# Splitting the last step of a weight conversion: rounding or storing two attention steps after the sign

## The chip, the cores and the metric

The kernel runs on one core of a Trainium2 chip. The core has a matrix engine (PE, TensorE), a vector engine (DVE, VectorE), a scalar engine (ACT, ScalarE), a general engine (POOL, GpSimd) and a queue that issues DMA transfers (SP, SyncE). Each engine runs its own instructions in the order in which the program emits them, and waits for other engines through semaphores. The metric is the device time of one launch in microseconds.

## The reference

Inputs are eight batches with eight heads, 576 positions and 64 features per head. The reference has three stages, all in float32:

```python
# 1. linear attention with positive features, per batch and head
proj = einsum('bhsd,df->bhsf', x, w_phi); proj -= max(abs(proj), axis=-1)
phi  = concat([exp(proj), exp(-proj)])
num  = phi(q) @ (phi(k).T @ v);  den = phi(q) . sum(phi(k)) + 1e-6
x    = num / den
# 2. causal convolution gate with 5 taps
x    = (sigmoid(conv5(x, conv_w)) * (x @ w_val)) @ w_out
# 3. Fourier mixing, layer norm, two-layer network
u    = x + real(fft2(x));  un = (u - mean) / sqrt(var + 1e-6)
out  = u + relu(un @ w_ch1) @ w_ch2
```

The weights `w_val`, `conv_w`, `w_out`, `w_ch1` and `w_ch2` arrive as float64 and are needed as float32 values, which the kernel makes on the chip from the two 32-bit halves of each number.

## The kernel before

The attention is cut into 16 units (a pair of batches and a pair of heads), each into five groups of 64-row or 128-row chunks, so 80 steps. `run_attention` (L1162) writes out one step after another by hand, and each step works on several groups at once: the projections of group `st` on PE (`emit_P`, L204, tile `pj`), the maximum and subtraction of group `st - 1` on DVE (`emit_Y`, L211 and L214), the key exponentials of group `st - 1` on ACT (`emit_kE`, L222 and L223, tile `ke`), the key-value products of group `st - 2` on PE (`emit_KV`, L243, tile `kv`), and so on. What is emitted first runs first on its engine. The third group of a unit is half as large; its projections show as `x8` instead of `x16`, so two such rows in succession are five steps apart.

Between these, the steps of the weight conversions are taken (`todo`). There are 21 pieces: two of `w_val` (tiles `wv`), two of `w_out` (`wo`), the small one of the taps, and 16 of `w_ch1` and `w_ch2`. One piece is a generator, `convert`, with four steps. The first loads the float64 numbers (L86, tile `raw`, two buffers). The second takes the exponent bits on DVE (L94) and the low half on ACT (L95). The third takes the high mantissa bits on DVE (L97, tile `mt`, two buffers), scales the exponent on ACT (L98) and does two operations on POOL (L99, L100). The fourth makes the sign on ACT (L102), multiplies twice on POOL (L103, L104) and calls `done`. For `w_val` and `w_out`, `done` rounds on ACT (L66, reading what L104 wrote) and subtracts on POOL (L75); for `w_ch1` and `w_ch2` it is a store on SP (L326, tile `w_scr`); for the taps a small copy on POOL (L347).

The four steps of piece `i` run at its start step plus 0, 3, 4 and 6, which is the table `lead`. The start is `i * (X_AT - 2 - lead[-1]) // 20`, with `X_AT` = 72, so `i * 64 // 20`: 0, 3, 6, 9, 12, 16, 19, 22 and so on to 64.

After the attention follow the gate and the Fourier mixing (batch by batch), and the two-layer network, whose order a planner chooses from its own costs.

Of the kernel before, what the change touches and what calls it, by code (L numbers as in the profile page):

```python
# [29 lines left out]
def f32(ap):  # L30
    return ap.bitcast(F32)
# [3 lines left out]
def attention_moe_mixer_kernel(  # L35
# [48 lines left out]
    def convert(i, src, n, shape, halve, done):  # L84
        raw = P["xf"].tile([128, 1024, 2], I32, tag="xf", name="raw64")[:, 0:n]
        nc.sync.dma_start(out=raw.rearrange("p n t -> p (n t)").rearrange("p (k f) -> p k f", k=shape[0]), in_=src)  # L86
        yield
        lo32, hi32 = raw[:, :, 0].bitcast(U32), raw[:, :, 1]
        a = P["xh"].tile([128, 2, 1024], I32, tag=f"x{i % 2}", name="cv")
        ex, lo = a[:, 0, 0:n], f32(a[:, 1, 0:n])  # L90
        sg = lo
        mt = stg.tile([128, 1024], I32, tag="mt", name="mt")[:, 0:n]
        w = f32(mt)
        nc.vector.tensor_scalar(out=ex, in0=hi32, scalar1=0x7FF00000, scalar2=None, op0=ALU.bitwise_and)  # L94
        nc.scalar.activation(out=lo, in_=lo32, func=ACTF.Copy, scale=2.0 ** -32)  # L95
        yield
        nc.vector.tensor_scalar(out=mt, in0=hi32, scalar1=0xFFFFF, scalar2=0x4B000000, op0=ALU.bitwise_and, op1=ALU.bitwise_or)  # L97
        nc.scalar.activation(out=ex, in_=ex, func=ACTF.Relu, scale=8.0, bias=ebias[:, int(halve):int(halve) + 1])  # L98
        nc.gpsimd.tensor_scalar(out=w, in0=w, scalar1=-7340032.0, scalar2=None, op0=ALU.add)  # L99
        nc.gpsimd.tensor_tensor(out=w, in0=lo, in1=w, op=ALU.add)  # L100
        yield
        nc.scalar.activation(out=sg, in_=hi32, func=ACTF.Sign)  # L102
        nc.gpsimd.tensor_tensor(out=w, in0=w, in1=f32(ex), op=ALU.mult)  # L103
        nc.gpsimd.tensor_tensor(out=w, in0=w, in1=sg, op=ALU.mult)  # L104
        done(w.rearrange("p (k f) -> p k f", k=shape[0]))
        yield

# [85 lines left out]
    def emit_P(i):  # L193
        u, g = divmod(i, NG)
        cs = GROUPS[g]
        n = len(cs)
        t = raw[u][0]
        pj[i] = p = ps_pj.tile([128, 2, 512], F32, tag="pj", name="pj")
        for w in range(2):
            for j, c in enumerate(cs):  # L200
                for h in range(2):
                    r = slice(64 * h, 64 * h + 64)
                    o = (w * n + j) * F
                    mm(p[:, h, o:o + F], t[r, w, 128 * c:128 * c + 128], wp[r, :], start=True, stop=True)  # L204

    def emit_Y(i, x):
        n = len(GROUPS[i % NG])
        pv = pj.pop(i)[:, :, 0:2 * n * F].rearrange("p h (c f) -> p h c f", f=F)
        m = sm_p.tile([128, 2, 2 * n], F32, tag="m", name="m")
        y = y_p.tile([128, 2, 2 * n, F], F32, tag="y", name="y")  # L210
        nc.vector.tensor_reduce(out=m, in_=pv, axis=AX.X, op=ALU.max, apply_absolute_value=True)  # L211
        if x is not None:
            emit_X(x)
        nc.vector.tensor_tensor(  # L214
            out=y, in0=pv, in1=m.unsqueeze(3).to_broadcast([128, 2, 2 * n, F]), op=ALU.subtract
        )
        yq[i] = y
# [40 lines left out]
    def emit_yT(i):  # L258
        n = len(GROUPS[i % NG])
        y = yq.pop(i)  # L260
        t = ps_tr.tile([128, 2, n, 128], F32, tag="tr", name="yt")
        for h in range(2):
            for j in range(n):
                nc.tensor.transpose(t[:, h, j, :], y[:, h, n + j, :], ident)
        e = qe_p.tile([128, 2, 2, n, 128], F32, tag="qe", name="qe")
        nc.scalar.activation(out=e[:, 0], in_=t, func=ACTF.Exp)
        nc.scalar.activation(out=e[:, 1], in_=t, func=ACTF.Exp, scale=-1.0)
        qE[i] = e
# [29 lines left out]
    def emit_XT(i):  # L298
        u, g = divmod(i, NG)
        bp, hp = divmod(u, 4)  # L300
        cs = GROUPS[g]
        n = len(cs)
        x = xs.pop(i)
        t = ps_tr.tile([128, n, 128], F32, tag="tr", name="xt")
        for j in range(n):
            nc.tensor.transpose(t[:, j, :], x[:, j].rearrange("p h d -> p (h d)"), ident)
        if g == 0:
            xT[u] = xT_p.tile([128, 2 * S], F32, tag="xT", name="xT")
        o = xT[u][:, 128 * cs[0]:128 * (cs[0] + n)]
        nc.scalar.activation(out=o, in_=t.rearrange("p c s -> p (c s)"), func=ACTF.Copy)  # L310
        if g == NG - 1:
            for b in range(2):
                nc.sync.dma_start(out=x_scr[2 * bp + b][hp], in_=xT[u][:, b * S:(b + 1) * S])
            xT.pop(u)
# [98 lines left out]
    def tap_steps(b, m):  # L413
        x = xf[b]
        if "psa" in P:
            acc = P["psa"].tile([128, 2, 512], F32, tag="pa", name="acc")[:, :, 0:HS]
        else:
            acc = P["g"].tile([128, 2, HS], F32, tag="acc", name="acc")

        def shifted(t):  # L420
            return x[:, m, t:t + S].rearrange("p (a s) -> p a s", a=2)
        nc.scalar.activation(out=acc, in_=shifted(4), func=ACTF.Copy, scale=cw[:, m, 4:5])  # L422
        for t in range(4):
            nc.vector.scalar_tensor_tensor(  # L424
                out=acc, in0=shifted(t), scalar=cw[:, m, t:t + 1], in1=acc, op0=ALU.mult, op1=ALU.add
            )
            if t < 3:
                yield
        taps[b, m] = acc
        yield  # L430

    def emit_taps(b, m):
        drain(tap_steps(b, m))
# [459 lines left out]
    def chain(*gens):  # L893
        for g in gens:
            yield from g
# [264 lines left out]


    def run_attention():  # L1162
        lead = (0, 3, 4, 6)
        todo = {}
        tap0 = chain(tap_steps(0, 0), tap_steps(0, 1))
        taps_at = (TOT - 4, TOT - 3, TOT - 2, TOT - 1, TOT, TOT, TOT + 1, TOT + 1)
        for i in range(len(pieces)):
            for l in lead:
                todo.setdefault(i * (X_AT - 2 - lead[-1]) // (len(pieces) - 1) + l, []).append(pieces[i])
        n_t = 2 * len(tables)  # L1170
        did_t = 0
        with tc.manual_schedule():
            for st in range(TOT + 6):
                u, g = divmod(st, NG)

                def at(lag):
                    return 0 <= st - lag < TOT

                if at(2):
                    emit_yT(st - 2)  # L1180
                if at(7) and st < TOT + 2:
                    emit_XT(st - 7)
                if at(0):
                    emit_P(st)
                if at(1):
                    emit_Y(st - 1, st - 6 if at(6) else None)
                elif st == TOT + 1:
                    emit_X(st - 6)
                if at(6) and st > TOT:
                    emit_XT(st - 6)  # L1190
                for c in todo.get(st, ()):
                    next(c)
                if at(1):
                    emit_kE(st - 1)
                if at(2):
                    emit_KV(st - 2)
                    emit_kvT(st - 2)
                for _ in range(taps_at.count(st)):
                    next(tap0)
                if at(5):  # L1200
                    emit_num(st - 5)
                    if st > TOT:
                        emit_X(st - 5)
                if g == (1 if u else 0) and u + 1 < NU:
                    load_kq(u + 1)
                if g == 2 and u + 1 < NU:
                    load_v(u + 1)
                while did_t < n_t and did_t * (X_AT - 5) < (st - 3) * n_t:
                    next(tables[did_t // 2])
                    did_t += 1  # L1210
                if st == X_AT:
                    assert did_t == n_t
                    load_x(0)
                    load_x(1)
                if 0 <= st - X_AT - 4 < 4:
                    split_x(0, (st - X_AT - 4,))
                if st == TOT + 1:
                    early.close()
                    open_mix()
                if 1 <= st - TOT < 5:  # L1220
                    emit_V(0, st - TOT - 1)
                    if st - TOT in (1, 3):
                        emit_taps(0, (st - TOT + 3) // 2)
# [145 lines left out]
```

## Time and profile before

| | |
|---|---|
| median of 3 runs | 1435.16 us (1435.16 to 1440.01) |
| the profiled execution | 1437.34 us, its span 1435.5 us |
| busy: PE, DVE, ACT, POOL | 94%, 87%, 57%, 49% |
| attention, 0 to 312 us | PE busy 286.16 us of 312 |
| the rest, 312 to 1435.5 us | PE busy 1060.96 us of 1123.5 |

A timeline row gives the start, the duration, the engine, the line, the operation with output and inputs, the sizes and the count of equal instructions that were merged; in square brackets stands the idle time of the engine just before, and the instruction that ended it. A row of the table by stretches gives, for each engine, its busy time and (in brackets) its number of instructions, then the granted PE clock as a share of 2.4 GHz, the share of time in which the DMA engines were busy, and the rate.

### The profile page before, as it was taken

To read this page: it belongs to the slowest core of one execution; us is meant where nothing else is said; L and a number is where in the kernel's file an instruction comes from. 1 tells how busy PE (TensorE), PEld (TensorE's weight loads), DVE (VectorE), ACT (ScalarE), POOL (GpSimd) and SP (SyncE) were. 2 spreads that over 40 slices of the span, in tenths; PEclk is the share of its full clock that TensorE was granted. 3 is DMA by queue.
4 is the path that set the end of the run, shared out by engine and by line. 5 is a ranking of instruction groups with operands and counts; after the bars stand their busy time and mean duration, and the time that the engine had idled before them with its cause. 6 is when DMAs were issued, how large, how long until landed. Compare 5 with 4: busy or idle time off the path is not lost.

```text
span 1435.5 us, 35040 instructions
## 1 busy us (share of the span) xinstructions
PE 1347.1 (94%) x14672; PEld 1297.1 (90%) x14672; DVE 1242.7 (87%) x1938; ACT 814.7 (57%) x1513; POOL 706.0 (49%) x526
## 2 busy tenths in 40 slices
PE   6899999997999999986899899999999999999998
PEld 6788888886999999976799899999999999999998
DVE  6689989876899999797999999999899887788876
ACT  5778888764545545464555554555465555444442
POOL 3858887732667666563555555545425111111111
PEclk9899999999999999998999999999999999999999
DMA  6347777741334433336323232222332222222211
GB/s 244 137 182 256 273 266 278 245 169 41 133 133 144 144 134 107 109 109 212 121 82 118 90 111 82 96 97 89 123 124 97 89 74 78 71 89 89 89 40 50
DMA packets 89851, 186.98 MB, mean 130 GB/s; under 512 B 10455, under 2 KB 37335, under 8 KB 87518
## 3 DMA queue, kind: packets, MB, share of 16 engines
q1 hardware_dynamic: 88488, 181.33, 37.2%
q10 hardware_dynamic: 1206, 3.41, 0.6%
q8 instruction: 115, 1.88, 0.5%
q14 instruction: 42, 0.34, 0.1%
HBM read 121.79 MB, written 62.93 MB: 129 GB/s over the span
## 4 chain that ended last, share of the span: by engine, by line
PE 43%; DVE 30%; POOL 9%; issue 8%; ACT 5%; DMA 4%; SPq 0%; ACTq 0%; DVEq 0%; POOLq 0%
PE cx L875 9%; PE x L806 9%; PE cy L875 5%; PE y L806 4%; DVE acc L424 4%; DVE A L647 3%; DVE c L647 3%; PE z L806 3%; PE kv L243 2%; DVE acc L647 2%; PE cz L875 2%; DMA raw<-in_w_ch_dram 2%; DVE s L751 2%; PE nm L282 2%; PE pj L204 2%
## 5 line engine op out<-in xcount | busy, mean ns | idle before, releaser
L875 PE MATMUL cx<-h,w 128*128 128x256 f32 x1152 | 176.2, 286 | 4.8 <-ACT h L66 2.5
L875 PEld LDWEIGHTS cx<-h,w 128*128 128x128 f32 x1152 | 158.3, 194 | 6.7 <-ACT h L66 3.1
L66 ACT ACTIVATE h<-c 128x512 fp32r<-128x512 f32 x180 | 111.6, 627 | 38.6 <-DVE c L647 22.2
L647 POOL TENSOR_TENSOR c<-c,c 128x512 f32<-128x512 f32 x35 | 49.7, 1421 | 167.9 <-ACT h L650 128.2
L647 DVE TENSOR_TENSOR acc<-cx,acc 128x512 f32<-128x512 f32 x144 | 98.1, 681 | 32.9 <-PE cx L875 32.2
L650 ACT ACTIVATE c<-c 128x512 f32<-128x512 f32 x108 | 67.9, 630 | 100.6 <-DVE c L647 99.3
L806 PE MATMUL x<-un,w 128*128 128x256 f32 x864 | 117.0, 285 | 7.6 <-DVE eo L647 6.9
L875 PE MATMUL cy<-h,w 128*128 128x256 f32 x864 | 117.3, 284 | 4.6 <-DVE h L72 1.9
L75 POOL TENSOR_TENSOR h<-c,h 128x512 fp32r<-128x512 f32 x33 | 48.1, 1459 | 148.9 <-ACT h L66 148.7
L806 PEld LDWEIGHTS x<-un,w 128*128 128x128 f32 x864 | 109.9, 193 | 8.2 <-issue 7.1
L424 DVE SCALAR_TENSOR_TENSOR acc<-xf,cw,acc 128x576 f32<-128x576 f32 x128 | 105.0, 820 | 11.9 <-ACT acc L422 10.6
L875 PEld LDWEIGHTS cy<-h,w 128*128 128x128 f32 x864 | 108.9, 191 | 7.0 <-DVE h L72 2.5
L243 PE MATMUL kv<-vraw,ke 128*64 128x66 f32 x2560 | 97.6, 230 | 14.6 <-ACT ke L222 9.8
L243 PEld LDWEIGHTS kv<-vraw,ke 128*64 128x64 f32 x2560 | 85.1, 141 | 26.2 <-ACT ke L222 13.2
L72 DVE TENSOR_TENSOR h<-c,h 128x512 fp32r<-128x512 f32 x111 | 104.2, 940 | 1.3 <-ACT h L66 0.7
L211 DVE TENSOR_REDUCE m<-pj 128x8 f32<-128x1024 f32 (+1 forms) x80 | 88.7, 1108 | 10.6 <-PE pj L204 10.6
L204 PE MATMUL pj<-wp,kqraw 64*128 64x128 f32 x1152 | 89.4, 294 | 5.7 <-DMA kqraw<-in_k_dram 4.9
L204 PEld LDWEIGHTS pj<-wp,kqraw 64*128 64x128 f32 x1152 | 73.8, 194 | 19.6 <-issue 18.1
L214 DVE TENSOR_TENSOR y<-pj,m 128x1024 f32<-128x1024 f32 (+1 forms) x80 | 88.7, 1109 | 0.4
L282 PE MATMUL nm<-kvT,qe 128*64 128x65 f32 x2304 | 84.4, 225 | 2.8 <-issue 1.3
L75 POOL TENSOR_TENSOR ge<-gs,ge 128x580 fp32r<-128x580 f32 x32 | 46.7, 1460 | 76.1 <-ACT ge L66 76.1
L99 POOL TENSOR_SCALAR mt<-mt 128x1024 f32<-128x1024 f32 (+1 forms) x21 | 55.6, 2650 | 57.4 <-DVE mt L97 47.3
(249 smaller groups left out, 4222.4 us busy)
## 6 DMA issues: line engine op xcount, KB each, us to landing
raw<-in_w_ch_dram SPq DMA_DIRECT2D x16, 1024.0 KB, 8.2
wr<-w_scr SPq DMA_DIRECT2D x32, 448.0 KB, 3.4
vraw<-in_v_dram SPq DMA_DIRECT2D x16, 660.0 KB, 9.3
x_scr<-xT SPq DMA_DIRECT2D x32, 288.0 KB, 6.5
xf<-x_scr SPq DMA_DIRECT2D x8, 1152.0 KB, 5.9
out_dram<-acc SPq DMA_DIRECT2D x36, 256.0 KB, 2.2
kqraw<-in_k_dram SPq DMA_DIRECT2D x15, 576.0 KB, 8.3
kqraw<-in_q_dram SPq DMA_DIRECT2D x15, 576.0 KB, 7.4
```

Source lines behind the costliest of these rows:

```text
L66: nc.scalar.activation(out=dst, in_=src, func=ACTF.Copy)
L72: nc.vector.tensor_tensor(out=dst, in0=src, in1=f32(hi), op=ALU.subtract)
L75: nc.gpsimd.tensor_tensor(out=dst, in0=src, in1=f32(hi), op=ALU.subtract)
L204: mm(p[:, h, o:o + F], t[r, w, 128 * c:128 * c + 128], wp[r, :], start=True, stop=True)
L211: nc.vector.tensor_reduce(out=m, in_=pv, axis=AX.X, op=ALU.max, apply_absolute_value=True)
L214: nc.vector.tensor_tensor(out=y, in0=pv, in1=m.unsqueeze(3).to_broadcast([128, 2, 2 * n, F]), op=ALU.subtract)
L243: mm(t[p, w, :], e[:, a, h, j, p], tv[:, h, slot, :], start=slot % 5 == 0 and w == 0, stop=slot % 5 == 4 and w == 3, skip_group_check=True)
L282: mm(t[p, 2 * j + h, 0:65], e[:, a, h, j, p], kt[:, 2 * h + a, b, :], start=(a == 0), stop=(a == 1))
L424: nc.vector.scalar_tensor_tensor(out=acc, in0=shifted(t), scalar=cw[:, m, t:t + 1], in1=acc, op0=ALU.mult, op1=ALU.add)
L647: op(e, cols, lambda e: (nc.vector if e == "v" else nc.gpsimd).tensor_tensor(out=o, in0=x, in1=y, op=alu), r, w)
L806: mm(p[:, n], l, v[:, kt], start=first and n + kt + m == 0, stop=kt == 1 and m == 2, skip_group_check=True)
L875: mm(p[:, o], v, r[:, n], start=first and o + n + m == 0, stop=n + m == 3, skip_group_check=True)
```

## The change

The call of `done` gets a step of its own, two attention steps behind the step that makes the sign, and `lead` grows by an entry.

```diff
@@ convert @@
         nc.scalar.activation(out=sg, in_=hi32, func=ACTF.Sign)
         nc.gpsimd.tensor_tensor(out=w, in0=w, in1=f32(ex), op=ALU.mult)
         nc.gpsimd.tensor_tensor(out=w, in0=w, in1=sg, op=ALU.mult)
+        yield
         done(w.rearrange("p (k f) -> p k f", k=shape[0]))
         yield
@@ run_attention @@
-        lead = (0, 3, 4, 6)
+        lead = (0, 3, 4, 6, 8)
```

Since `lead[-1]` is in the formula for the start steps, these become `i * 62 // 20`: 0, 3, 6, 9, 12, 15, 18, 21, 24, 27, 31 and so on to 62. The first five are as before; later pieces start up to two steps earlier, and their last step stays at 70 at the latest. The order of instructions on PE is the same in both kernels.

On ACT, at steps 6 to 8 (the sign of piece 0 is L102 of `raw_226`; lines below L105 count one more in the changed kernel). Before:

```order
L102 ACTIVATE cv<-raw_226 128x1024
L66 ACTIVATE wv_147<-mt 128x1024
L95 ACTIVATE cv<-raw_311 128x1024
L222 ACTIVATE ke<-y 128x512
L223 ACTIVATE ke<-y 128x512
L66 ACTIVATE sq<-tab 128x580
L266 ACTIVATE qe<-yt 128x512
```

On ACT, the same place in the changed kernel:

```order
L102 ACTIVATE cv<-raw_226 128x1024
L95 ACTIVATE cv<-raw_311 128x1024
L223 ACTIVATE ke<-y 128x512
L224 ACTIVATE ke<-y 128x512
L66 ACTIVATE sq<-tab 128x580
L267 ACTIVATE qe<-yt 128x512
L268 ACTIVATE qe<-yt 128x512
L311 ACTIVATE xT<-xt 128x256
L98 ACTIVATE cv<-cv,ebias 128x1024
L223 ACTIVATE ke<-y 128x512
L224 ACTIVATE ke<-y 128x512
L267 ACTIVATE qe<-yt 128x512
```

The rounding `wv<-mt` no longer stands between the sign and the next two key exponentials; it comes 13 instructions later, in step 8.

On POOL, from the first piece on, before (L99 to L104 are the arithmetic of one piece, L75 the subtraction behind the rounding):

```order
L99 TENSOR_SCALAR mt<-mt 128x1024
L100 TENSOR_TENSOR mt<-cv,mt 128x1024
L103 TENSOR_TENSOR mt<-mt,cv 128x1024
L104 TENSOR_TENSOR mt<-mt,cv 128x1024
L75 TENSOR_TENSOR wv_148<-mt,wv_147 128x1024
L99 TENSOR_SCALAR mt<-mt 128x1024
L100 TENSOR_TENSOR mt<-cv,mt 128x1024
L103 TENSOR_TENSOR mt<-mt,cv 128x1024
```

On POOL, the same place in the changed kernel:

```order
L99 TENSOR_SCALAR mt<-mt 128x1024
L100 TENSOR_TENSOR mt<-cv,mt 128x1024
L103 TENSOR_TENSOR mt<-mt,cv 128x1024
L104 TENSOR_TENSOR mt<-mt,cv 128x1024
L99 TENSOR_SCALAR mt<-mt 128x1024
L100 TENSOR_TENSOR mt<-cv,mt 128x1024
L75 TENSOR_TENSOR wv_148<-mt,wv_147 128x1024
L103 TENSOR_TENSOR mt<-mt,cv 128x1024
```

The subtraction of one piece has moved behind the first two operations of the next.

On SP, where the stores of the third and fourth piece of `w_ch1` and `w_ch2` stand, before:

```order
L326 DMA w_scr_73<-mt 128x2x512
L86 DMA raw_2024<-in_w_ch_dram 128x2x1024
L313 DMA x_scr_67<-xT 128x576
L313 DMA x_scr_68<-xT 128x576
L326 DMA w_scr_74<-mt 128x2x512
```

On SP, the same two stores in the changed kernel:

```order
L86 DMA raw_1962<-in_w_ch_dram 128x2x1024
L191 DMA vraw<-in_v_dram 128x1320
L327 DMA w_scr_73<-mt 128x2x512
L314 DMA x_scr_67<-xT 128x576
L314 DMA x_scr_68<-xT 128x576
L86 DMA raw_2242<-in_w_ch_dram 128x2x1024
L186 DMA kqraw<-in_k_dram 128x1152
L186 DMA kqraw<-in_q_dram 128x1152
L354 DMA tab<-in_feat_tab_dram 128x516
L327 DMA w_scr_74<-mt 128x2x512
```

Each store now stands behind the load of the piece after next, and not ahead of it.

## Rows read from the trace of the kernel before

**Rows 1.** The page, part 1: busy us, share of the span, instructions.
```profile
PE 1347.1 (94%) x14672; PEld 1297.1 (90%) x14672; DVE 1242.7 (87%) x1938; ACT 814.7 (57%) x1513; POOL 706.0 (49%) x526
```
**Rows 2.** Table by stretches; columns: stretch, length, PE, PEld, DVE, ACT, POOL, clock, DMA.
```profile
21.80:82.85 61.05, 50.54 (x993) 44.87 (x992) 41.47 (x72) 42.76 (x79) 49.85 (x23) 0.92 0.36 127
34.14:38.50 4.36, 4.18 (x59) 3.59 (x60) 1.21 (x4) 4.36 (x9) 4.28 (x3) 0.67 0.67 272
49.14:53.00 3.86, 3.73 (x65) 3.47 (x65) 0.16 (x1) 3.79 (x7) 3.86 (x2) 0.56 0.23 89
...
85.85:295.36 209.51, 202.54 (x4372) 181.23 (x4371) 189.36 (x323) 174.13 (x330) 162.23 (x67) 1.00 0.74 258
276.83:295.36 18.53, 18.34 (x404) 16.61 (x403) 15.70 (x30) 14.64 (x30) 10.80 (x6) 1.00 0.51 183
```
**Rows 3.** Timeline of ACT, 27 to 79 us: the four roundings L66.
```profile
31.47 1.06 ACT L66 ACTIVATE wv<-mt 128x1024 fp32r<-128x1024 f32 x1 [3.24 <-POOL mt L104]
...
46.48 1.06 ACT L66 ACTIVATE wv<-mt 128x1024 fp32r<-128x1024 f32 x1 [2.57 <-POOL mt L104]
...
62.53 1.06 ACT L66 ACTIVATE wo<-mt 128x1024 fp32r<-128x1024 f32 x1 [2.53 <-POOL mt L104]
...
77.89 1.06 ACT L66 ACTIVATE wo<-mt 128x1024 fp32r<-128x1024 f32 x1 [2.53 <-POOL mt L104]
```
**Rows 4.** Timeline of PE, 29 to 87 us.
```profile
29.88 0.72 PE L204 MATMUL pj<-wp,kqraw 64*128 64x128 f32 x8
34.14 0.34 PE L243 MATMUL kv<-vraw,ke 128*64 128x66 f32 x4 [3.55 <-ACT ke L222]
...
49.14 2.33 PE L243 MATMUL kv<-vraw,ke 128*64 128x66 f32 x32 [1.90 <-ACT ke L222]
...
57.68 0.72 PE L204 MATMUL pj<-wp,kqraw 64*128 64x128 f32 x8
...
65.18 0.34 PE L243 MATMUL kv<-vraw,ke 128*64 128x66 f32 x4 [3.33 <-ACT ke L222]
...
79.63 0.34 PE L243 MATMUL kv<-vraw,ke 128*64 128x66 f32 x4 [1.05 <-ACT ke L222]
...
82.85 0.71 PE L204 MATMUL pj<-wp,kqraw 64*128 64x128 f32 x8
...
86.94 1.15 PE L243 MATMUL kv<-vraw,ke 128*64 128x66 f32 x32
```
**Rows 5.** Timeline of POOL, 32 to 47 us: one whole piece.
```profile
32.60 2.79 POOL L75 TENSOR_TENSOR wv<-mt,wv 128x1024 fp32r<-128x1024 f32 x1 [1.17 <-ACT wv L66]
35.36 2.77 POOL L99 TENSOR_SCALAR mt<-mt 128x1024 f32<-128x1024 f32 x1
38.21 2.36 POOL L100 TENSOR_TENSOR mt<-cv,mt 128x1024 f32<-128x1024 f32 x1
40.65 2.36 POOL L103 TENSOR_TENSOR mt<-mt,cv 128x1024 f32<-128x1024 f32 x1
44.05 2.39 POOL L104 TENSOR_TENSOR mt<-mt,cv 128x1024 f32<-128x1024 f32 x1 [1.04 <-ACT cv L102]
```
**Rows 6.** Timeline of DVE: the bit operations of two early pieces.
```profile
32.48 0.68 DVE L97 TENSOR_SCALAR mt<-raw 128x1024 int32<-128x1024 int32 x1
...
43.55 0.68 DVE L94 TENSOR_SCALAR cv<-raw 128x1024 int32<-128x1024 int32 x1
```
**Rows 7.** Line L94 up to 330 us: durations in ns, minimum, median, maximum.
```profile
L94 DVE TENSOR_SCALAR cv<-raw x21: 167/1425/2615, 15.0 to 278.6; 128x1024 int32<-128x1024 int32 x20, 128x20 int32<-128x20 int32 x1
```
**Rows 8.** Waits, 82 to 300 us: total us, times, longest.
```profile
DVE cv L94 <- DMA raw<-in_w_ch_dram: 4.4, 8, 1.0
```
**Rows 9.** Waits of SP's own queue, 0 to 330 us.
```profile
SPq L326 <- POOL mt L104: 119.8, 16, 11.8
```
**Rows 10.** Line L326 (stores), then line L86 (loads): us from issue to landing.
```profile
DMA to landing us min/median/max: 2.9/3.2/4.5
...
DMA to landing us min/median/max: 2.3/8.0/9.5
```

## Prediction

> **What bounds the kernel now.** I read the page's busy shares first: PE works 94% of the span [rows 1], so a change that adds or takes no matmul can only pay where PE waits or runs at its lower clock. The table by stretches says where that is. In the attention's later stretch, 85.85 to 295.36 us, PE is busy 202.54 of 209.51 us at full clock; in 21.8 to 82.85 us it is busy 50.54 of 61.05 us and the clock is 0.92 [rows 2]. The conversions whose last step moves lie in both.
>
> The timeline of PE shows what the early loss is made of. Four times the key-value products wait for the key exponentials of ACT: 3.55, 1.90, 3.33 and 1.05 us, together 9.83 us [rows 4]. The timeline of ACT shows why those exponentials are late: the four roundings of `w_val` and `w_out` stand in ACT's queue ahead of them, and each holds the queue for 2.53 to 3.24 us until POOL has finished L104 of the same piece [rows 3]. It ends at 31.47, 46.48, 62.53 and 77.89 us, and PE's waits end 1.7 to 2.7 us later each time.
>
> Behind a wait PE also runs slower. In the 4.36 us after the first the granted clock is 0.67, in the 3.86 us after the second 0.56 [rows 2], so part of each stretch ran at 1.2 and not 2.4 GHz; before it PE had stood still. The matmul time lost is (1 - 0.67) x 4.36 = 1.4 us and (1 - 0.56) x 3.86 = 1.7 us.
>
> The whole early loss comes from the half-sized projections, which are five steps apart. Two units take from 29.88 to 82.85 us, 52.97 us [rows 4]. A late unit, with conversions still running in part of it, takes 18.53 us [rows 2]. So 52.97 - 2 x 18.53 = 15.9 us are lost, of which 9.8 are the waits and most of the rest the clock.
>
> **The change part by part.** *Roundings on ACT, and subtractions on POOL.* Nothing is added or removed: four L66 on ACT of 1.06 us, four L75 on POOL, one small copy, 16 stores and their issues go two steps later. The wait of ACT for L104 in step 6, 9, 12 and 15 goes, since two steps (7.4 us at 18.53 / 5 = 3.7 each) pass before the rounding comes up. With no other limit PE gets back the 15.9 us. But what is late next is POOL. One piece of `w_val` or `w_out` costs it, from start to start: L75 2.76 us, L99 2.85, L100 2.44, L103 2.36 and L104 2.39 with about 0.08 between, together 12.9 us [rows 5], while three steps of PE take 11.1. So POOL falls behind by 1.8 us a piece, and it cannot go back further than its start.
>
> I follow POOL's queue. Its second piece can start when DVE has written the mantissa, 32.48 + 0.68 = 33.2 us [rows 6]; that is two us earlier than before, as the subtraction no longer stands ahead of it. Three pieces later, at 33.2 + 3 x 12.9 = 71.9 us, L104 of the fourth piece ends. Then follow its rounding (1.06 us) and the first key exponential (0.6 us), and the key-value products of step 18 can start at 73.6 us. Before, they start at 86.94 us [rows 4]. POOL therefore allows 13.3 us of the 15.9. On the way ACT's signs of the third and fourth piece have to wait for POOL's L100 (the sign overwrites what L100 reads): the queue gives L100 of the third piece at 33.2 + 12.9 + 5.3 = 51.4 us, about 2 us after ACT is there. That wait lies inside the 2.6 us by which POOL is the slower; one more stretch at 1.2 GHz behind it does not quite, so I take 0.8 us off (half of the 1.7 above). The early part gives 12.5 us, between 5 (rival one) and 15.9.
>
> *A rule against it.* DVE's bit operations L94 take 0.68 us where POOL stands idle beside them [rows 6] and up to 2.62 us elsewhere [rows 7]. The change fills POOL's idle times in the early part, so L94 and L97 of the third and fourth piece may grow by up to 1.9 us each; DVE is busy 41 of 61 us there [rows 2], which hides it, and I price it at nothing; with that cover gone it is 4 x 1.9 = 7.6 us (rival four). The Trainium skill (SBUF — State Buffer, section "SBUF: two separate sides") says that VectorE and GpSimd share a pair of ports as an exclusive lock: whichever starts first keeps it for its whole instruction, and the other fully blocks. By that rule the growth is certain where an instruction of POOL is under way, and only its cover is open; the trace's 0.68 and 2.62 us agree with it.
>
> *Stores on SP.* SP's queue stood 119.8 us in 16 waits for L104, each with later loads behind it [rows 9]. These waits go, and the loads of the next pieces are issued before the store and not after. What PE could see of it is small: DVE waited 4.4 us, in eight waits, for the loaded weights [rows 8]. Over 85.85 to 295.36 us, 54 steps, the loss against 18.53 us a unit is 209.5 - 10.8 x 18.53 = 9.4 us, and those 4.4 are in it, partly hidden. I take 1.5 us of gain. The upper bound is 6 of the 9.4 us. On the lower side, the pieces come every 3.1 steps and not 3.2. One costs DVE 1.4 + 0.7 = 2.1 us [rows 6, 7], so the conversions' 50-odd steps each carry 0.02 us more, 1.1 us if DVE set the pace; with stores that land later (rival three's beginning), -3.
>
> *The rest.* From step 70 on nothing is changed: its time is carried over.
>
> *Sum.* 12.5 + 1.5 = 14.0 us off the profiled execution's 1437.3 us gives 1423.3. That execution lay 2.2 us above the median of 1435.16, so against the medians I say 1421.
>
> **The rivals.** *One: the wait only changes its place.* POOL's load is the same, so ACT may wait for L100 at the sign where it waited for L104 at the rounding. For it speaks 12.9 us of POOL work against 11.1 us of steps. Against it, POOL also stood idle in each early cycle, 1.17 and 1.04 us in the piece shown [rows 5], because ACT was held, and that idle time goes. If three sign waits of 2 us each cost PE 1.7 us more by the clock, 11 of the 15.9 us stay lost: a gain of 5, 1430 us.
>
> *Two: more comes back.* If the freed SP queue also takes away most of the later loss, the gain is 13.3 + 6 = 19, or 1416 us. For it speaks that DVE, busy 189 of 209 us there [rows 2], has little room to absorb the waits for the loads; against it, the longest such wait is 1.0 us [rows 8].
>
> *Three: slower, by the buffers `mt`.* There are two, and the store must have read one before DVE's L97 of the piece after next may write it. With the store at step 8 and pieces three steps apart, two steps, 7.4 us, are left; before it was four. Stores landed in 2.9 to 4.5 us when they stood ahead of the loads; the loads took 8.0 in the middle and 9.5 at most [rows 10]. If a store behind a load lands as late as that, L97 waits up to 2.1 us in each of 14 pieces, 29 us in all, against 12.5 won: 17 slower, 1452 us. It decides from 0.9 us a piece on. Against it, the store can be issued ahead of its step, as soon as L104 is done and the queue has come to it.
>
> *Four: DVE's bit operations grow on PE's path.* With the 7.6 us above, 12.5 + 1.5 - 7.6 = 6.4 us are won, 1429 us. For it speaks that L97 stands ahead of the next maximum in DVE's queue; against it, that the early DVE is idle a third of the time.
>
> **How the numbers follow.** The forecast has 0.55, rival one 0.13, rival two 0.20, rival three 0.08, rival four 0.04. About 0.5%, 7.2 us, is what a measurement of this kernel can tell from no change. The forecast and rival two are faster by more; of rival one 0.05 lies beyond it, the rest within, as does rival four; of rival three 0.01 is within and 0.07 slower. So 0.80, 0.13 and 0.07. The range reaches from 1411 (15.9 + 6 = 22 gained, and a little) to 1431 (a gain of 4, rival one): what is left out is the worse half of rival one, rival three and a tail of rival two, under 0.2. The likeliest case by itself has 1417 to 1426.
>
> **What would show it.** In the changed kernel's ACT timeline the four roundings have waits under 1.5 us and there is no wait of PE for key exponentials above 2.5 us before step 18; the key-value products that started at 86.94 us start near 74. POOL runs without gaps from 33 to 72 us. SP has almost no wait for L104, and DVE waits for loads under 2 us. I am wrong if ACT's waits stand at the signs with 2 us or more each, or if DVE's L97 or POOL's L99 waits for stores.

## The result and the profile after

The changed kernel took 1424.83 us (median of six runs, 1419.57 to 1427.96) and the kernel before 1435.51 us in the same session. The medians lie 10.7 us apart. The ratio of paired runs is 0.991, with a 95% interval of 0.9891 to 0.993: 12.9 us less, between 10.0 and 15.6. A later session gave 1423.37 us against 1439.29, a ratio of 0.9888 (0.987 to 0.9906). The forecast was 1421 us, from a gain of 14.0 us.

The profiled execution after is at 1427.96 us the slowest of its six, with a span of 1426.1 us. First the early part. The stretch of [rows 2], with the same edges, and then the two early units alone:

```profile
21.80:82.85 61.05, 57.48 (x1227) 50.84 (x1223) 58.20 (x92) 51.12 (x97) 52.70 (x26) 1.00 0.57 202
28.50:69.00 40.50, 38.22 (x807) 33.83 (x806) 38.95 (x63) 34.69 (x66) 37.57 (x16) 1.00 0.53 187
```

and the two units in the kernel before:

```profile
29.88:82.85 52.97, 42.46 (x807) 37.50 (x806) 33.70 (x63) 37.92 (x70) 42.01 (x20) 0.90 0.40 144
```

PE, in the first column behind the length, is busy 57.48 us where it was 50.54, and the clock is 1.00 where it was 0.92. DVE, the third, is busy 58.20 us where it was 41.47; in the two units alone, 38.95 of 40.50 us, where the same 63 instructions took 33.70 of 52.97. In the timeline of PE, three half-sized projections, five steps apart each, frame the two units:

```profile
28.46 0.72 PE L205 MATMUL pj<-wp,kqraw 64*128 64x128 f32 x8
...
47.65 1.16 PE L283 MATMUL nm<-kvT,qe 128*64 128x65 f32 x32 [0.75 <-DVE xs L294]
...
49.55 0.71 PE L205 MATMUL pj<-wp,kqraw 64*128 64x128 f32 x8
...
69.12 0.72 PE L205 MATMUL pj<-wp,kqraw 64*128 64x128 f32 x8
...
75.14 1.15 PE L244 MATMUL kv<-vraw,ke 128*64 128x66 f32 x32
```

They take 69.12 - 28.46 = 40.66 us, against 52.97 [rows 4]: 12.3 us less. No wait for key exponentials is among them; the longest wait that is left, 0.75 us, is for DVE. The key-value products of step 18 start at 75.14 us and not at 86.94 [rows 4]. ACT's timeline has the four roundings, and the sign that waits longest (of the others here, that of the second piece waits 0.36 us and that of the third not at all):

```profile
33.92 1.08 ACT L66 ACTIVATE wv<-mt 128x1024 fp32r<-128x1024 f32 x1
...
46.04 1.07 ACT L66 ACTIVATE wv<-mt 128x1024 fp32r<-128x1024 f32 x1
...
58.87 1.06 ACT L66 ACTIVATE wo<-mt 128x1024 fp32r<-128x1024 f32 x1 [0.47 <-POOL mt L104]
...
64.06 1.16 ACT L102 ACTIVATE cv<-raw 128x1024 f32<-128x1024 int32 x1 [1.86 <-POOL mt L100]
...
71.17 1.06 ACT L66 ACTIVATE wo<-mt 128x1024 fp32r<-128x1024 f32 x1 [0.80 <-POOL mt L104]
...
72.66 0.61 ACT L224 ACTIVATE ke<-y 128x512 f32<-128x512 f32 x1
```

Waits of 2.53 to 3.24 us [rows 3] have become 0, 0, 0.47 and 0.80. The last row is the key exponential that the products of step 18 read. On POOL, as forecast, the second piece starts at 32.30 us and little stands between its instructions from there on; L104 of the fourth piece ends at 71.14, where 71.9 was worked out:

```profile
32.30 2.77 POOL L99 TENSOR_SCALAR mt<-mt 128x1024 f32<-128x1024 f32 x1 [1.80 <-ACT ke L223]
...
37.46 2.38 POOL L75 TENSOR_TENSOR wv<-mt,wv 128x1024 fp32r<-128x1024 f32 x1
...
42.71 2.37 POOL L104 TENSOR_TENSOR mt<-mt,cv 128x1024 f32<-128x1024 f32 x1
...
50.90 2.38 POOL L75 TENSOR_TENSOR wv<-mt,wv 128x1024 fp32r<-128x1024 f32 x1
53.24 2.82 POOL L103 TENSOR_TENSOR mt<-mt,cv 128x1024 f32<-128x1024 f32 x1
...
68.78 2.36 POOL L104 TENSOR_TENSOR mt<-mt,cv 128x1024 f32<-128x1024 f32 x1
```

The bit operations of DVE in the same time, of which the prediction thought that they may grow without being seen:

```profile
31.52 0.68 DVE L97 TENSOR_SCALAR mt<-raw 128x1024 int32<-128x1024 int32 x1
37.87 2.53 DVE L94 TENSOR_SCALAR cv<-raw 128x1024 int32<-128x1024 int32 x1
43.65 1.98 DVE L97 TENSOR_SCALAR mt<-raw 128x1024 int32<-128x1024 int32 x1
51.89 1.94 DVE L94 TENSOR_SCALAR cv<-raw 128x1024 int32<-128x1024 int32 x1
55.54 1.07 DVE L97 TENSOR_SCALAR mt<-raw 128x1024 int32<-128x1024 int32 x1
62.87 1.20 DVE L94 TENSOR_SCALAR cv<-raw 128x20 int32<-128x20 int32 x1
66.98 1.76 DVE L97 TENSOR_SCALAR mt<-raw 128x20 int32<-128x20 int32 x1
```

At 0.68 us each the first five would take 3.4 us; they take 8.2. The last two, of the taps, have 20 elements a partition and take 1.20 and 1.76 us, where such an L94 took 0.17 at the least [rows 7].

For the stores, the waits of SP's queue and of DVE up to 330 us (total, times, longest) answer to [rows 8, 9]:

```profile
SPq L327 <- POOL mt L104: 23.2, 10, 7.6
...
DVE cv L94 <- DMA raw<-in_w_val_dram: 0.8, 1, 0.8
DVE mt L97 <- DMA w_scr<-mt: 0.2, 1, 0.2
```

and the landing times, of the stores and then of the loads, to [rows 10]:

```profile
DMA to landing us min/median/max: 4.8/9.4/10.9
...
DMA to landing us min/median/max: 2.1/5.9/10.3
```

SP waited 23.2 us for L104, not 119.8. DVE no longer waits for any load of `w_ch1` or `w_ch2`, where it waited 4.4 us. The stores land in 9.4 us in the median, three times later than before, and yet L97 waited only 0.2 us for one.

Over the whole span: the first half-sized projection of the second unit stands 1.4 us earlier (28.46 and 29.88; in the other profiles it stands between 27.0 and 29.5, at 27.3 and 27.5 in the two that keep the old order up to there, so this is scatter), the two units give 12.3 us, the twelve units after them take 233.4 us instead of 231.9, and what follows 1123.5 instead of 1120.8. That is 1.4 + 12.3 - 1.6 - 2.8 = 9.4 us by unrounded figures, the difference of the spans. The two losses have to be looked at: either the change costs something there, or it is scatter.

### The profile page after: what moved, and what is told of

Same layout as the page of the kernel before. It is cut to its first block, busy times and chain, and to the rows that moved or that the text cites. A ratio compares the mean times of both kernels' runs of the same rounds, so it can differ in the third digit from the quotient of the medians.

```text
span 1426.1 us, 35034 instructions
## 1 busy us (share of the span) xinstructions
PE 1346.5 (94%) x14672; PEld 1296.2 (91%) x14672; DVE 1254.0 (88%) x1938; ACT 814.0 (57%) x1513; POOL 706.9 (50%) x526
## 4 chain that ended last, share of the span: by engine, by line
PE 48%; DVE 34%; issue 6%; ACT 4%; POOL 4%; DMA 3%; SPq 0%; DVEq 0%; POOLq 0%; ACTq 0%
PE cx L876 9%; PE x L807 9%; PE cy L876 5%; PE y L807 4%; PE kv L244 4%; DVE acc L425 4%; PE pj L205 3%; DVE A L648 3%; DVE c L648 3%; PE nm L283 3%; PE z L807 3%; DVE acc L648 2%; PE cz L876 2%; DVE y L215 2%; DVE s L752 2%
## 5 line engine op out<-in xcount | busy, mean ns | idle before, releaser
L66 ACT ACTIVATE h<-c 128x512 fp32r<-128x512 f32 x180 | 111.6, 627 | 38.9 <-DVE c L648 22.4
L648 POOL TENSOR_TENSOR c<-c,c 128x512 f32<-128x512 f32 x35 | 49.8, 1422 | 165.0 <-ACT h L651 125.4
L75 POOL TENSOR_TENSOR h<-c,h 128x512 fp32r<-128x512 f32 x33 | 48.3, 1466 | 149.2 <-ACT h L66 148.9
L75 POOL TENSOR_TENSOR ge<-gs,ge 128x580 fp32r<-128x580 f32 x32 | 46.8, 1461 | 78.7 <-ACT ge L66 78.7
L283 PEld LDWEIGHTS nm<-kvT,qe 128*64 128x64 f32 x2304 | 76.5, 140 | 9.6 <-issue 7.7
```

Of the source, the lines that this page charges most:

```text
L66: nc.scalar.activation(out=dst, in_=src, func=ACTF.Copy)
L75: nc.gpsimd.tensor_tensor(out=dst, in0=src, in1=f32(hi), op=ALU.subtract)
L283: mm(t[p, 2 * j + h, 0:65], e[:, a, h, j, p], kt[:, 2 * h + a, b, :], start=(a == 0), stop=(a == 1))
L648: op(e, cols, lambda e: (nc.vector if e == "v" else nc.gpsimd).tensor_tensor(out=o, in0=x, in1=y, op=alu), r, w)
```

## The experiments

Three questions were put. Does the early gain come from the roundings on ACT? What do the stores and the closer start steps give by themselves? And what still holds the two early units at 40.7 us, where 37.06 us (two units of 18.53 [rows 2]) would do?

**Roundings alone, stores alone, starts alone.** Five kernels take the change apart. In the first only the pieces that are rounded (and the taps) get the step of their own:

```diff
-        yield
+        if i < 5:
+            yield
         done(w.rearrange("p (k f) -> p k f", k=shape[0]))
+        if not (i < 5):
+            yield
```

> Only the first five pieces (the four that round on ACT, and the taps) have their last step two attention steps later; the 16 stores stay with the sign, as before. Start steps as in the changed kernel (i*62//20). Theory A (the whole gain is ACT no longer held by four roundings): 1422 to 1426 us, the two early units take about 41 us, and the stretch after them is up to 3 us shorter than in the changed kernel. Rival B (the freed SP queue gives part of it): 1428 to 1432 us.

It took 1427.97 us against 1438.42, ratio 0.9936 (0.9919 to 0.9953). Its timeline of PE has the two units in 68.14 - 27.43 = 40.71 us:

```profile
27.43 0.71 PE L208 MATMUL pj<-wp,kqraw 64*128 64x128 f32 x8
...
68.14 0.71 PE L208 MATMUL pj<-wp,kqraw 64*128 64x128 f32 x8
```

So the early gain is that of the roundings, whole. The total is above the 1422 to 1426 us that my theory gave and just short of rival B's 1428, so the stores with the sign cost more than the theory had them cost.

The counterpart, `i >= 5` in place of `i < 5`, leaves the roundings with the sign and moves the stores:

> Only the 16 stores go two attention steps later; the roundings stay with the sign. Start steps as in the changed kernel. Theory A: no gain, 1434 to 1439 us, the two early units take about 53 us as before, and SP's waits for POOL are gone all the same. Rival B: 1428 to 1432 us.

1437.85 us, ratio 0.9994 (0.9979 to 1.0009). The two units take 54.07 us:

```profile
27.32 0.72 PE L208 MATMUL pj<-wp,kqraw 64*128 64x128 f32 x8
...
81.39 0.71 PE L208 MATMUL pj<-wp,kqraw 64*128 64x128 f32 x8
```

and in its waits the old one of PE stands again, 10.2 us in four pieces:

```profile
PE kv L247 <- ACT ke L226: 10.2, 4, 4.0
```

The third is the kernel before with the new start steps:

```diff
-                todo.setdefault(i * (X_AT - 2 - lead[-1]) // (len(pieces) - 1) + l, []).append(pieces[i])
+                todo.setdefault(i * (X_AT - 2 - 8) // (len(pieces) - 1) + l, []).append(pieces[i])
```

> The kernel before, with the start steps of the changed kernel (i*62//20 instead of i*64//20) and nothing else. Theory A: 1435 to 1438 us, no gain or a loss of up to 2 us from conversions that stand closer together. Rival C (the earlier starts give part of the gain): 1428 to 1433 us.

1439.87 us, ratio 1.0016 (1.0 to 1.0033): nothing, or a loss of a few us at most. The two units take 51.61 us. Against it the stores of the run before can be weighed, since both have the same starts, the same program in the early part and the same session: 0.9994 against 1.0016 is 3.2 us, the medians alone 2.0. The two intervals still touch. The two units, 54.07 and 51.61 us by the same program, show how far single profiles scatter here.

The fourth has late roundings, stores with the sign, and the old starts (the first diff, and `- 6` in the start formula):

> The roundings two steps later, stores with the sign, and the start steps of the kernel before (i*64//20): the smallest edit that takes ACT's four waits away. Theory A: 1421 to 1425 us, the same or 1 to 3 us better than the changed kernel. If the closer starts are needed (rival C) it is 1428 us or more.

1429.94 us, ratio 0.9941 (0.992 to 0.9961); two units in 40.70 us. Again the early part is as expected and the total 5 us above the upper end, where rival C had it. But the first kernel has the closer starts and the same ratio (0.9936), so the starts are not the cause. Its waits of DVE from 70 to 312 us show what the old place of the stores does:

```profile
DVE cv L94 <- DMA raw<-in_w_ch_dram: 6.8, 6, 2.2
```

The other two kernels with the stores at the sign have 4.0 us (roundings alone) and 6.6 us (starts alone) in this row; the kernels with late stores have none.

The fifth has everything late and the old starts, and with it the changed kernel was run again:

> Roundings and stores two steps later as in the changed kernel, but the start steps of the kernel before (i*64//20). If the closer starts cost about 2 us (as e4 against before suggests) and the late stores win about 3 (as e2 against e4), this is 1 to 3 us faster than the changed kernel in the same job, with the two early units at about 41 us. Rival: the starts do nothing and e4 was chance; then it is within 1 us of the changed kernel.

> The changed kernel once more, timed beside the others of this job: 9 to 13 us below the kernel before; the two early units take 40 to 42 us in its profile. Its stretch after them tells how far the 233.4 us of the first profile was chance.

1423.92 us, ratio 0.9891 (0.9874 to 0.9908), and 1423.37, 0.9888 (0.987 to 0.9906). They are the same, as the rival had it, so the closer start steps do nothing that can be measured. The repeat also settles the loss in the later attention: its twelve units take 229.72 us, not 233.43, with the same program. The difference is time in which PE waits for nothing that the profile shows. From 70 to 312 us the first profile after has

```profile
PE nm L283 <- issue: 4.1, 4, 1.7
PE pj L205 <- issue: 1.8, 2, 1.1
```

and the repeat

```profile
PE nm L283 <- issue: 0.9, 1, 0.9
```

Single profiles scatter by this much, so I take means. The twelve units take 230.6 us in four profiles with late stores (228.53, 229.72, 230.68, 233.43) and 233.6 in four with the stores at the sign (231.75, 231.86, 233.95, 236.82): 3.0 us, with an overlap. Four more kernels with late stores, which otherwise differ in the first pieces only and come next, have 228.5 to 229.9 us.

**What holds the early units.** Candidates are DVE, whose bit operations had grown, and POOL, for which two signs still wait. The first kernel leaves L94 out for the first five pieces:

```diff
-        nc.vector.tensor_scalar(out=ex, in0=hi32, scalar1=0x7FF00000, scalar2=None, op0=ALU.bitwise_and)
+        if i >= 5:
+            nc.vector.tensor_scalar(out=ex, in0=hi32, scalar1=0x7FF00000, scalar2=None, op0=ALU.bitwise_and)
...
-        nc.scalar.activation(out=ex, in_=ex, func=ACTF.Relu, scale=8.0, bias=ebias[:, int(halve):int(halve) + 1])
+        nc.scalar.activation(out=ex, in_=ex if i >= 5 else hi32, func=ACTF.Relu, scale=8.0, bias=ebias[:, int(halve):int(halve) + 1])
```

> The changed kernel without DVE's L94 (the mask of the exponent bits) for the first five pieces; ACT's L98 reads the loaded word itself, so the exponent of these weights is not computed. Theory D (DVE, with bit operations lengthened beside POOL, sets the early pace): the two early units fall from 40.7 to 37.5 to 39 us, total 1 to 3 us below the changed kernel. Theory P (POOL's queue sets it, as predicted): 40 to 41 us, total unchanged.

The two units take 66.75 - 28.57 = 38.18 us, 2.5 less:

```profile
28.57 0.71 PE L206 MATMUL pj<-wp,kqraw 64*128 64x128 f32 x8
...
66.75 0.72 PE L206 MATMUL pj<-wp,kqraw 64*128 64x128 f32 x8
```

ACT's sign waits for POOL as before, twice and 1.9 us at the longest:

```profile
ACT cv L103 <- POOL mt L101: 2.2, 2, 1.9
```

So most of the rest hangs on DVE's L94. The median, 1423.26 us (ratio 0.989, 0.987 to 0.9909), shows nothing of the 2.5 us: in its profile the part after the attention is 1.5 us longer than in the repeat, and between all profiles of this study that part, whose program is the same, takes from 1119.6 to 1127.1 us.

The opposite test takes work from POOL and gives it to DVE, the four subtractions L75:

```diff
-            lo_pool(w[1][:, k], t, w[0][:, k])
+            lo_dve(w[1][:, k], t, w[0][:, k])
```

> The changed kernel with the subtraction L75 of the four rounded pieces on DVE instead of POOL (four instructions, the same result). Theory P: POOL's piece falls from 12.9 to about 10.3 us, less than three steps, and the two early units take 38 to 39.5 us. Theory D: DVE has no room, they take 41.5 to 44 us and the total is 1 to 3 us above the changed kernel.

The two units took 69.48 - 27.58 = 41.90 us, 1.2 longer, though POOL had less to do:

```profile
27.58 0.71 PE L205 MATMUL pj<-wp,kqraw 64*128 64x128 f32 x8
...
69.48 0.71 PE L205 MATMUL pj<-wp,kqraw 64*128 64x128 f32 x8
```

Its median was 1426.36 us, ratio 0.9906 (0.9887 to 0.9926), 3.0 us above the changed kernel's. This falls on the side of DVE. Next, L94 and POOL's offset L99 are both left out for the first five pieces, in one run:

```diff
-        nc.gpsimd.tensor_scalar(out=w, in0=w, scalar1=-7340032.0, scalar2=None, op0=ALU.add)
+        if i >= 5:
+            nc.gpsimd.tensor_scalar(out=w, in0=w, scalar1=-7340032.0, scalar2=None, op0=ALU.add)
```

> For the first five pieces both L94 on DVE and L99 on POOL (the subtraction of the constant) are left out, so these weights come out wrong in exponent and offset. In e7, without L94 alone, the two early units took 38.2 us and ACT still waited 1.9 us at a sign for POOL's L100. If POOL is what is left after DVE, this falls to 37.0 to 37.6 us; if it stays at 38 or more, something else is next.

37.33 us (28.94 to 66.27), and neither ACT nor PE waits for POOL any more: POOL's own share was 38.18 - 37.33 = 0.85 us at most, since DVE's three mantissa operations of this stretch took 0.5 us less in this run, too. Then all bit operations are back, and POOL's four operations L99, L100, L103 and L104 are left out for the four rounded pieces:

```diff
-        nc.gpsimd.tensor_scalar(out=w, in0=w, scalar1=-7340032.0, scalar2=None, op0=ALU.add)
-        nc.gpsimd.tensor_tensor(out=w, in0=lo, in1=w, op=ALU.add)
+        if i >= 4:
+            nc.gpsimd.tensor_scalar(out=w, in0=w, scalar1=-7340032.0, scalar2=None, op0=ALU.add)
+            nc.gpsimd.tensor_tensor(out=w, in0=lo, in1=w, op=ALU.add)
...
-            hi_act(w[0][:, k], t)
+            nc.scalar.activation(out=w[0][:, k], in_=t, func=ACTF.Copy, scale=2.0 ** -23)
```

(L103 and L104 likewise; L75 now subtracts the rounded value from itself.)

> For the four rounded pieces POOL's L99, L100, L103 and L104 are left out (the rounding scales the mantissa word by 2**-23 instead and the subtraction gives zeros, so these weights are wrong); DVE's L94 and L97 stay. If DVE's bit operations are long because POOL works beside them, all of them fall to 0.7 us for the early pieces and the two early units take 37 to 38 us. If they are long for another reason (the strided read, ACT's reads of the same buffer), they keep their 1.9 to 2.8 us and the units take 39 us or more.

37.20 us, and DVE's timeline has every bit operation of the rounded pieces at 0.68 to 0.77 us:

```profile
35.28 0.77 DVE L94 TENSOR_SCALAR cv<-raw 128x1024 int32<-128x1024 int32 x1
...
39.30 0.69 DVE L97 TENSOR_SCALAR mt<-raw 128x1024 int32<-128x1024 int32 x1
...
47.23 0.68 DVE L94 TENSOR_SCALAR cv<-raw 128x1024 int32<-128x1024 int32 x1
...
49.62 0.68 DVE L97 TENSOR_SCALAR mt<-raw 128x1024 int32<-128x1024 int32 x1
```

That shows it of the bit operations: they were long because they stood beside POOL's work. The table by stretches has PE busy for all of the two units:

```profile
26.99:64.19 37.20, 37.17 (x808) 33.36 (x807) 32.17 (x62) 34.56 (x67) 6.17 (x5) 1.00 0.63 216
```

The 40.66 - 37.20 = 3.5 us are what the lengthened operations and POOL's own queue cost together, since this kernel takes both away. It and the one before were executed once each (1414.73 and 1423.62 us), so only their timelines are used.

**Two that missed.** If DVE holds the early units, it might hold the later ones too. This kernel leaves L94 out for all 21 pieces:

```diff
-        nc.vector.tensor_scalar(out=ex, in0=hi32, scalar1=0x7FF00000, scalar2=None, op0=ALU.bitwise_and)
...
-        nc.scalar.activation(out=ex, in_=ex, func=ACTF.Relu, scale=8.0, bias=ebias[:, int(halve):int(halve) + 1])
+        nc.scalar.activation(out=ex, in_=hi32, func=ACTF.Relu, scale=8.0, bias=ebias[:, int(halve):int(halve) + 1])
```

> L94 left out for all 21 pieces (ACT's L98 reads the loaded word, so the exponents are wrong). If DVE sets the pace of the later attention too, the 12 units after the early two fall from 229.7 us (the changed kernel's second profile) to 220 to 226 us; a unit without any wait would give 12 x 18.33 = 220. If POOL or the DMAs set it, 228 to 231 us. What follows after the attention isn't compared.

This kernel was executed once (1420.35 us). The early part came out as expected, 38.15 us, but the twelve later units take 295.11 - 66.43 = 228.68 us, within the other kernels' scatter and not 220 to 226:

```profile
66.43 0.71 PE L204 MATMUL pj<-wp,kqraw 64*128 64x128 f32 x8
...
295.11 0.72 PE L204 MATMUL pj<-wp,kqraw 64*128 64x128 f32 x8
```

So DVE's time for L94 does not set the pace there. What does, the runs leave open.

The last kernel was meant to beat both. It moves L94 to stand directly ahead of L97, so that one wait for POOL's instruction would serve both:

```diff
-        nc.vector.tensor_scalar(out=ex, in0=hi32, scalar1=0x7FF00000, scalar2=None, op0=ALU.bitwise_and)
         nc.scalar.activation(out=lo, in_=lo32, func=ACTF.Copy, scale=2.0 ** -32)
         yield
+        nc.vector.tensor_scalar(out=ex, in0=hi32, scalar1=0x7FF00000, scalar2=None, op0=ALU.bitwise_and)
         nc.vector.tensor_scalar(out=mt, in0=hi32, scalar1=0xFFFFF, scalar2=0x4B000000, op0=ALU.bitwise_and, op1=ALU.bitwise_or)
```

> The changed kernel with L94 one step later, directly ahead of L97, where POOL has just run out of work and waits for L97; the same results. If POOL's instructions lengthen L94, its mean falls from 1.77 to about 0.9 us, DVE gains about 15 us over the attention, and the total falls by 3 to 8 us below the changed kernel (ratio to the kernel before 0.983 to 0.987). Against it: ACT's L98 reads what L94 writes and now waits about 1 us for it in the same step, which could cost as much; then 0.987 to 0.991.

1423.5 us, ratio 0.9887 (0.986 to 0.9914): the changed kernel's time. The early units take 43.66 us, 3 longer, and PE waits 3.6 us there for an operation of DVE, where the profile after has 1.3:

```profile
PE nm L283 <- DVE xs L294: 3.6, 2, 2.4
```

DVE's timeline shows why it is late (L96 is now the first of the two bit operations):

```profile
42.06 1.31 DVE L96 TENSOR_SCALAR cv<-raw 128x1024 int32<-128x1024 int32 x1
43.29 2.86 DVE L97 TENSOR_SCALAR mt<-raw 128x1024 int32<-128x1024 int32 x1
```

and POOL's beside it:

```profile
40.43 2.39 POOL L103 TENSOR_TENSOR mt<-mt,cv 128x1024 f32<-128x1024 f32 x1
42.90 2.70 POOL L104 TENSOR_TENSOR mt<-mt,cv 128x1024 f32<-128x1024 f32 x1
```

The first ends at 43.37, just behind L103 (42.82); by then POOL's next instruction is under way, and the second has to sit that out too, until 46.15. Two in a row pay twice. The wait of ACT's L98 that the expectation had against it came too, 2.5 us in three, but PE waited for ACT 0.5 us in all.

## Why the prediction was right

*The early loss and its cause* held. Taking the four roundings out of ACT's queue gives 12.3 us by the first two profiles. The five profiles that have it and change nothing else in this part take 40.66 to 40.71 us for the two units, the three without it 51.61 to 54.07, so by any pair it is 10.9 to 13.4. Rival one, the wait that only moves to the sign, did happen in small: 1.86 us once, at the fourth piece and not at the third, and POOL's whole share was 0.85 us at most.

*The size of that term*, 12.5 us, was right for a reason that was partly wrong. The prediction put the 2.6 us that do not come back on POOL's queue and 0.8 on the clock. POOL's queue did run as worked out (71.14 us against 71.9), but it did not hold PE at the end: the key exponentials of step 18 were done at 73.27, and their products start at 75.14 without a wait. The clock stayed at 1.00. Of the 3.6 us left above 37.06, leaving L94 out gave 2.5 and relieving POOL as well 0.85. That 12.5 met 12.3 is in this respect luck. The step that failed is "DVE is busy 41 of 61 us there, which hides it, and I price it at nothing". That was the DVE of a kernel whose PE stood still. With those waits gone the same work falls into less time: the 33.70 us that DVE took in the two units before would leave 3.4 of 37.06 us free, and it grew by 5.25, to 38.95 of 40.50 us. The cover was made of the very waits that the change takes away. Rival four was thus present. The operations of the third and fourth piece grew by 4.8 us over 0.68 each, against a bound of 7.6, and those of the taps, which the prediction did not count, by 2.6. What the growth cost the runs do not give by itself: the 2.5 us contain the 0.68 us that each L94 takes alone, and leave the growth of L97 in; together with POOL's queue it is 3.5 us.

*Stores.* 1.5 us were forecast, with 6 as the upper bound. Within one session the runs give 2.0 to 3.2 us, with intervals that touch. The changed kernel against the first one, with the roundings alone, gives more: 0.9936 against 0.991 and 0.9888 is 3.7 and 6.9 us, though from different sessions. So the term was sized too small. The mechanism fits: the waits for loads, 4.0 to 6.8 us with the stores at the sign, are gone in every kernel with late stores. That they were hidden less than the prediction took them to be is likely, and no run shows it.

*Rival three* saw the landing times rightly (9.4 us in the median, as late as the loads) and the consequence wrongly: L97 waited 0.2 us. SP still waits for L104 at ten of the sixteen stores, 23.2 us in all, which is more than the "almost no wait" of the forecast. At these stores SP is there before POOL is done and issues them as soon as L104 ends, as the prediction had said against this rival.

*The sum.* The measured pieces, 3 us of them the stores by the twelve units, are 12.3 + 3 = 15 us against a forecast of 14.0. The two sessions give 12.9 (10.0 to 15.6) and 16.1 us (13.5 to 18.7). That the first profile after shows 9.4 is the issue stalls and the scatter behind the attention; no run explains what makes either, and that stays open.

## What to carry to other kernels

When an engine that waits for a second one holds up a third, move the waiting instruction to where its input is done, and then follow the queue of the second engine to see how much comes back. Do not cover a cost with idle time that exists only because of the stall you remove: count the engine's busy time over the shorter stretch that will be left. A store that waits at the head of a DMA queue delays the loads behind it, and that can be worth more than the wait of the store's buffer.

## What the runs showed of the hardware

How long DVE's bit operations take beside POOL can be worked out to a few hundredths of a us. In the profile after, L94 from 37.87 ends at 40.40, and the L75 of POOL that was under way ends at 39.84, 0.56 us before. L97 from 43.65 ends 0.55 us after L104 (45.08), L94 from 51.89 ends 0.55 after L75 (53.28), L97 from 55.54 ends 0.55 after L103 (56.06). In the last experiment the two ends lie 0.55 us behind POOL's L103 (42.82) and L104 (45.60). So the instruction of DVE stands until POOL's is over and then has 0.55 us to go; with POOL's arithmetic taken away it takes 0.68 to 0.77 us in all. It also goes the other way: the L97 of 0.68 us that [rows 6] shows began at 32.48 us, and POOL was not idle beside it, as the prediction read it, but began L75 0.12 us later. That L75 took 2.79 us [rows 5], where the two shown of the profile after take 2.38. The Trainium skill (SBUF — State Buffer, section "Who interferes with whom") says that a DVE operation in a two-port mode and a GpSimd instruction exclude each other, and that the one issued first keeps the shared pair for its whole length; these ends agree with it. The condition of the two-port mode is left out where the prediction calls the growth certain; the ends show that these bit operations do come under the rule. The two in a row of the last experiment show that the pair can go back to POOL in between.

Stores that are queued behind loads landed in 7.0 to 9.4 us, the medians of four profiles with late stores, and not in the 3.2 and 3.3 us of the four with the stores at the sign. And PE's idle time without a visible cause went from 0.9 to 5.9 us between two profiles of one program, more than one term of this sum.
